# Opening products spread over eight places of the array, two fillers instead of 43, and a new step order in a delta-rule attention and expert-attention kernel

## The chip, the cores and the metric

The kernel runs on one core of a Trainium2 chip. The metric is device time in microseconds (us) of one execution. Three executions of the kernel before took 444.64, 447.53 and 451.43 us; the median is 447.53 us. Engines are named as the profile names them: PE (matrix products; PEld is its weight loads), DVE (vector), ACT (scalar), POOL (GpSimd) and SP (which issues the DMA transfers).

## The reference

The first half is a delta-rule recurrence over 768 tokens, for 4 batches and 8 heads of width 48. The second half takes its output as `x` and runs four experts of causal attention, with the two best gates of each token kept.

```python
k_n = k / (norm(k) + 1e-6)
for t in range(768):
    y[t]  = q[t] @ state
    state = state + beta[t] * outer(k_n[t], v[t] - k_n[t] @ state)
x = y, heads side by side: (4, 768, 384)
w = softmax over the two best of x @ w_gate
for e in range(4):
    q, k, v = x @ wq[e], x @ wk[e], x @ wv[e]        # width 64
    a = softmax(0.125 * q @ k.T, causal)
    out += gate[e] * (a @ v @ wo[e])
```

## The kernel before, in words

The recurrence is done in blocks. The work is cut into six units `n` (two pairs of batches by three stretches of 256 tokens), and each unit into four chunks `c` of 64 tokens. For one chunk, `gram` forms the products of the keys with themselves, and the triangular system that they make is solved for 64 tokens at a time. Unit 0 is solved in pieces of 16 rows on DVE and put together by products on PE (`gram_up`, `diag`, `expand`); the other units are solved in pieces of 32 rows on POOL and put together by `merge1` and `merge2`. Then the chain `ks, u, q, s, y` carries the state through the four chunks, and projections, scores, maxima, values and the output product of the experts follow (`pj, pv, mx, mp, mr, sc, av, nm, ft, fo`).

No scheduler orders the instructions. Every piece of work is a named step (`gr0.2` is `gram(0, 2)`, `sv0.9` is step 9 of the solve of unit 0), and the string `ORDER` lists them; the loop at L744 issues them in that order on all engines, and each engine runs its own instructions in the order in which they were issued. `+9` stands for nine fillers: products of a zero tile, 128 rows by 256 columns in bfloat16, that nobody reads.

The steps that the prediction follows are these. `load_k`, `load_q` and `load_chain` (`lg`, `lq`, `lc`) start transfers on SP. `gr0.c` is 32 float32 products on PE (L242) and two DVE operations that carry them out (L248). `si` (L273) transposes on DVE; `pre` (L289 to L310) prepares the solve; `sv0` (L335, L336) runs on DVE, `sv1` to `sv5` (L332, L333) on POOL after the product of L306. `so` (L353) and `sn` (L350) transpose the solved blocks back. `dg` (L360 to L363) places them with ACT and POOL, `ex` (L373) multiplies them on PE, `gq` (L267, L269) is the product of keys and queries, and `gu` (L256, L259) the part of the Gram product above the 16-row pieces, carried out by ACT. `gr1.c` is carried out by ACT (L246). All products share four PSUM banks in turn, the tiles `pm__66` to `pm__69`.

Before `ORDER` begins, PE runs one filler and `MINI` = 40 small float32 products, 48 rows by 32 columns with 4 columns moving, all into one place (L129). One float32 product is issued as two weight loads and two products, so four instructions; a filler is two.

Of the kernel before, what the change touches and what calls it, by code (L numbers as in the profile page):

```python
# [38 lines left out]
sv0.4 sv0.5 sv0.6 gu2 sv0.7 sv0.8 ks0.0 gu3 sv0.9 +4 gu0 sv0.10 sv0.11 sv0.12 sv0.13 +17 gr1.1 sv0.14 +2 gu1 sv0.16
vt0.1 so0 lq1.1 sn0 gr1.2 +5 gr1.0 si1 pre1.0 dg1 gq1.0 dg0 pre1.1 pre1.2 pre1.3 dg2 +62 ex1.0 +2 gq0.1 ex0.0 +9 ex2.0  # L40
ex1.1 ex0.1 pre1.4 gq0.0 dg3 sv1.1 sv1.2 sv1.3 +1 ex0.2 gq0.2 sv1.4 +2 ex0.3 kc3 cb sv1.5 sv1.6 ex1.2 u0.0 sv1.7 sv1.8
ex3.0 s0.0 sv1.9 ex1.3 ks0.1 w0 w4 y0.0 vs0 sv1.10 lc0.2 sv1.11 sv1.12 vt0.2 sv1.13 sv1.14 lq1.2 ex2.1 +9 q0.1 kc0
u0.1 ex2.2 s0.1 gq0.3 w1 w3 sv1.15 sv1.16 ks0.2 kc2 lc0.3 sv1.17 vt0.3 ex2.3 sv1.18 y0.1 lq1.3 ex3.1 sv1.19 sv1.20 w2
sv1.21 w6 hx0.1.0 sv1.22 +1 q0.2 lg2.1 u0.2 lq2.0 lg2.2 ex3.2 +1 s0.2 +7 ks0.3 lg2.3 y0.2 ex3.3 pv0.0.1 sv1.23 gq1.2
q0.3 lc1.0 sv1.24 sv1.25 lg2.0 sv1.26 u0.3 gr2.1 y0.3 hx0.3.0 sv1.27 gr2.2 gr2.3 sv1.28 sv1.29 sv1.30 +1 gr2.0 sv1.31
s0.3 si2 pj0.0.0 sv1.32 vt1.0 lc1.1 vt1.1 pj0.0.2 so1 mv1.1 sn1 pv0.1.0 q1.0 lq2.2 ks1.0 pre2.0 pre2.1 mv1.0 vs1 vs2
pj0.1.0 kc1 +5 m11.0 mv1.2 pre2.2 pre2.3 m11.1 mv1.3 cl1 pj0.1.2 pre2.4 sv2.1 sv2.2 sv2.3 m21.3 lg3.0 m21.0 w5 pv0.0.0
gq1.1 u1.0 m21.2 lq2.1 sv2.4 s1.0 sv2.5 mx0.1.1.1 m21.1 ks1.1 mx0.1.0.0 y1.0 mx0.0.1.1 gr3.0 sv2.6 sv2.7 sv2.8 mp0.1
sv2.9 u1.1 lc1.2 q1.1 lq2.3 vt1.2 +2 s1.1 sv2.10 mx0.0.0.0 mp0.0 gq2.0 lg3.1 mr0.1 ks1.2 mr0.0 y1.1 sv2.11 sv2.12
pv0.1.1 lc1.3 u1.2 sv2.13 hx1.1.0 sv2.14 sv2.15 sv2.16 q1.2 gq1.3 gr3.1 s1.2 gt0 vt1.3 sv2.17 sv2.18 sc0.0.0.0 sv2.19  # L50
sc0.0.1.0 lg3.2 lc2.0 ks1.3 sv2.20 sv2.21 lq3.0 y1.2 lg3.3 pj1.0.0 q1.3 u1.3 gq2.1 gq2.3 y1.3 sc0.1.0.0 gr3.3 +3 gq3.0
gr3.2 av0.0.0 si3 av0.0.1 av0.1.1 av0.0.3 pj1.0.2 hx1.3.0 +1 pj1.1.0 pv1.0.1 sv2.22 s1.3 av0.1.0 sv2.23 sv2.24 sv2.25
pre3.0 av0.0.2 sv2.26 sv2.27 pre3.1 mx1.0.0.0 pre3.2 sv2.28 sv2.29 sv2.30 sv2.31 pre3.3 pj1.1.2 sv2.32 so2 vt2.0
pv1.0.0 sn2 pre3.4 q2.0 ks2.0 sc0.1.1.0 mv2.0 lg4.0 sv3.1 pv1.1.1 sv3.2 m12.0 m12.1 cl2 sv3.3 nm0.0 mx1.0.0.1 mv2.1
pv1.1.0 m22.0 mx1.1.1.2 mv2.2 av0.1.3 sv3.4 u2.0 mx1.1.1.3 lc2.1 mv2.3 av0.1.2 s2.0 m22.2 lc2.2 vt2.1 sv3.5 nm0.1
m22.1 lq3.2 m22.3 sv3.6 sv3.7 sv3.8 mx1.0.1.2 vt2.2 ks2.1 sv3.9 sv3.10 sv3.11 ft0.0 mx1.0.1.3 sv3.12 sv3.13 y2.0 u2.1
lq3.1 mx1.1.0.1 mp1.0 fo0.0.0 q2.1 lq3.3 s2.1 mr1.0 fo0.0.1 sv3.14 sv3.15 sv3.16 gq2.2 gq3.1 ks2.2 lg4.2 y2.1 sv3.17
gr4.0 lc2.3 u2.2 vt2.3 lq4.2 sv3.18 mx1.1.0.0 sc1.0.0.1 hx2.1.0 ft0.1 q2.2 sv3.19 mp1.1 sv3.20 s2.2 sc1.0.0.0 sv3.21
sv3.22 sc1.0.1.0 gt1 sv3.23 ks2.3 y2.2 gr4.2 pv2.0.0 lg4.3 sv3.24 sv3.25 mr1.1 lg4.1 pj2.0.0 sv3.26 lc3.0 sv3.27 q2.3
u2.3 gr4.3 gq3.2 y2.3 hx2.3.0 fo0.1.1 gq3.3 gr4.1 av1.0.0 av1.0.1 sc1.0.1.1 si4 lq4.0 sv3.28 sv3.29 sv3.30 pj2.0.2  # L60
pj2.1.0 sv3.31 sv3.32 fo0.1.0 vt3.0 mx2.0.1.4 so3 av1.0.3 sn3 av1.0.2 lq4.1 sc1.1.0.0 mv3.2 sc1.1.0.1 pv2.0.1 mv3.1
m13.0 mx2.0.0.0 lc3.1 mv3.0 av1.1.0 m23.0 m23.1 pre4.0 pre4.1 m13.1 ks3.0 nm1.0 pre4.2 pre4.3 cl3 pre4.4 sc1.1.1.1
vt3.1 ft1.0 pj2.1.2 sv4.1 mv3.3 sv4.2 sv4.3 lg5.0 sv4.4 u3.0 gr5.0 s3.0 mx2.0.1.5 mx2.0.0.1 ks3.1 y3.0 m23.2 pv2.1.0
sv4.5 u3.1 mx2.1.1.5 sv4.6 sv4.7 mx2.0.0.2 mx2.0.0.3 q3.1 s3.1 lc3.2 sc1.1.1.0 mx2.1.1.4 vt3.2 ks3.2 sv4.8 sv4.9
sv4.10 lg5.1 y3.1 sv4.11 sv4.12 sv4.13 lg5.2 mx2.0.1.6 lc3.3 vt3.3 sv4.14 mx2.0.1.7 sv4.15 hx3.1.0 pv2.1.1 u3.2 gr5.1
sv4.16 q3.2 s3.2 lc4.0 mp2.0 sv4.17 sv4.18 mx2.1.1.6 av1.1.1 av1.1.2 av1.1.3 mr2.0 fo1.0.1 sc2.0.0.2 m23.3 ks3.3 lg5.3
gq4.1 y3.2 sc2.0.0.0 sc2.0.0.1 q3.3 u3.3 sv4.19 nm1.1 mx2.1.0.0 mx2.1.0.1 sv4.20 sv4.21 sv4.22 +1 y3.3 av2.0.1 av2.0.0
mx2.1.0.2 mx2.1.0.3 lq5.1 sc2.0.1.1 gr5.3 sv4.23 vt4.0 s3.3 gr5.2 gq5.1 ks4.0 mx2.1.1.7 mp2.1 sv4.24 sv4.25 sv4.26 si5
pre5.0 pre5.1 sc2.0.1.2 sc2.0.1.0 sv4.27 mr2.1 fo1.0.0 av2.0.2 sv4.28 sv4.29 sv4.30 sv4.31 pre5.2 av2.0.3 sc2.1.0.1
sv4.32 sc2.1.0.2 pre5.3 pre5.4 sv5.1 so4 pv3.0.0 pj3.0.0 hx3.3.0 mv4.0 ft1.1 mv4.1 sv5.2 sv5.3 lq5.0 sv5.4 pj3.1.0  # L70
sc2.1.0.0 lc4.1 mv4.2 sv5.5 sv5.6 sv5.7 sn4 m14.0 av2.1.0 sv5.8 sv5.9 sv5.10 av2.1.1 gt2 lq4.3 nm2.0 sc2.1.1.1
sc2.1.1.2 m24.0 m24.1 m14.1 cl4 sv5.11 sv5.12 sv5.13 sc2.1.1.0 pj3.0.2 sv5.14 pj3.1.2 vt4.1 u4.0 sv5.15 sv5.16 sv5.17
sv5.18 sv5.19 gq4.0 q4.0 s4.0 av2.1.2 av2.1.3 mx3.0.0.0 mx3.0.1.1 fo1.1.1 mp3.0 pv3.0.1 lc4.2 ks4.1 y4.0 gq4.2 u4.1
gq4.3 vt4.2 lq5.2 q4.1 mv4.3 sv5.20 sv5.21 s4.1 mr3.0 sv5.22 pv3.1.1 sv5.23 sv5.24 sv5.25 lq5.3 nm2.1 mx3.1.1.1
fo1.1.0 ks4.2 y4.1 m24.3 sv5.26 lc4.3 vt4.3 m24.2 ft2.0 pv3.1.0 sv5.27 sv5.28 sv5.29 sv5.30 hx4.1.0 u4.2 gq5.0 sv5.31
sv5.32 q4.2 s4.2 sc3.0.0.0 lc5.0 mx3.1.0.0 mp3.1 vt5.0 ks4.3 y4.2 pv4.0.1 fo2.0.0 fo2.0.1 ft2.1 pj4.0.2 gq5.2 so5 sn5
mv5.2 q4.3 mv5.0 u4.3 mr3.1 fo2.1.0 mv5.3 y4.3 hx4.3.0 s4.3 sc3.0.1.0 mv5.1 m15.1 m15.0 pj4.0.0 ks5.0 m25.0 m25.1
m25.3 gt3 pv4.0.0 pj4.1.0 pj4.1.2 q5.0 cl5 u5.0 mx4.0.1.3 lc5.1 vt5.1 sc3.1.0.0 m25.2 s5.0 mx4.0.0.1 av3.0.0 ks5.1
mx4.1.1.3 mx4.1.0.1 y5.0 u5.1 av3.1.0 sc3.1.1.0 mx4.0.0.0 lc5.2 q5.1 s5.1 av3.0.2 vt5.2 av3.0.3 lc5.3 av3.0.1 av3.1.2
vt5.3 nm3.0 av3.1.1 mx4.0.1.2 mp4.0 gq5.3 ks5.2 y5.1 hx5.1.0 pv4.1.0 fo2.1.1 mr4.0 pv4.1.1 u5.2 mx4.1.1.2 sc4.0.0.1  # L80
q5.2 s5.2 sc4.0.0.0 sc4.0.1.1 gt4 ks5.3 y5.2 ft3.0 pj5.0.0 q5.3 u5.3 mx4.1.0.0 mx5.0.0.0 y5.3 av4.0.0 mp4.1 hx5.3.0
av3.1.3 mx5.1.0.0 sc4.0.1.0 pj5.0.2 nm3.1 fo3.0.0 mr4.1 fo3.0.1 mx5.0.0.1 pj5.1.2 ft3.1 pj5.1.0 av4.0.1 mx5.0.1.6
sc4.1.0.1 av4.0.2 mx5.0.1.5 av4.0.3 mx5.0.0.2 sc4.1.0.0 sc4.1.1.0 mx5.0.0.3 av4.1.0 av4.1.1 mx5.0.1.4 sc4.1.1.1
mx5.0.1.7 mp5.0 nm4.0 pv5.0.0 fo3.1.1 mr5.0 fo3.1.0 ft4.0 pv5.1.0 mx5.1.0.1 av4.1.2 mx5.1.1.6 sc5.0.0.2 fo4.0.0
mx5.1.1.5 av4.1.3 sc5.0.0.1 sc5.0.0.0 fo4.0.1 nm4.1 mx5.1.1.4 mx5.1.1.7 av5.0.0 mx5.1.0.2 sc5.0.1.2 av5.0.1 mx5.1.0.3
mp5.1 sc5.0.1.0 sc5.0.1.1 ft4.1 pv5.1.1 mr5.1 pv5.0.1 gt5 av5.0.2 sc5.1.0.2 av5.0.3 sc5.1.0.0 sc5.1.0.1 fo4.1.0 nm5.0
av5.1.0 sc5.1.1.0 av5.1.1 sc5.1.1.1 sc5.1.1.2 fo4.1.1 ft5.0 av5.1.2 av5.1.3 fo5.0.1 fo5.0.0 nm5.1 ft5.1 +12 fo5.1.0
# [4 lines left out]
def tile_kernel(ctx, tc, kq, kv, beta, wqk, wvg, wo, consts, out):
# [24 lines left out]
    def mm(o, a, b, start, stop=True):  # L117
        T.matmul(o, lhsT=a, rhs=b, start=start, stop=stop, skip_group_check=True)  # L118
# [696 lines left out]
```

## Time and profile before

The profiled execution took 448.62 us; its span, from the first to the last instruction, is 446.9 us.

| | us | share of the span |
|---|---|---|
| median of three executions | 447.53 | |
| profiled execution | 448.62 | |
| its span | 446.9 | |
| PE busy | 423.3 | 95% |
| DVE busy | 277.2 | 62% |
| POOL busy | 256.8 | 57% |
| ACT busy | 203.5 | 46% |

PE is busy nearly everywhere, but a filler counts as busy too, and the ends of products are modelled. POOL works from 46 us to about 345 us, on the solves of units 1 to 5. The first 50 us hold the solve of unit 0, which only DVE runs, and little of what PE does there is on the path. A bracket at the end of a timeline row gives the idle time before it and what ended that; "issue" means that nothing that the profile shows was being waited for.

### The profile page before, as it was taken

What the parts mean: (1) busy time and instruction counts of PE and PEld (TensorE: products, weight loads), DVE (VectorE), ACT (ScalarE), POOL (GpSimd) and SP (SyncE); (2) the same over time, 40 slices, a digit from 0 to 9 for tenths busy, and PEclk for the clock granted to TensorE, in tenths of its full rate; (3) what the DMA queues carried; (4) which work ended last, traced back from release to release, by engine and by line L of the source; (5) the groups of instructions that cost most, each with busy time, mean ns of one, the idle gap of its engine ahead of it and who ended that gap; (6) DMA issues with size and microseconds to landing.
All of it is one profiled execution on the core that took longest, in us unless ns stands there. A gap on an engine that the chain in (4) does not pass through costs nothing.

```text
span 446.9 us, 24375 instructions
## 1 busy us (share of the span) xinstructions
PE 423.3 (95%) x10935; PEld 381.7 (85%) x10935; DVE 277.2 (62%) x615; ACT 203.5 (46%) x555; POOL 256.8 (57%) x477
## 2 busy tenths in 40 slices
...
PEclk9869998799999966999999999999999999999999
...
GB/s 273 209 4 4 5 155 130 106 103 76 87 127 23 60 3 86 158 90 75 91 62 116 70 27 96 4 32 132 88 37 49 68 38 33 24 38 38 1 29 81
...
## 3 DMA queue, kind: packets, MB, share of 16 engines
q1 hardware_dynamic: 18864, 31.18, 22.2%
q8 instruction: 86, 1.41, 1.3%
...
## 4 chain that ended last, share of the span: by engine, by line
PE 79%; DVE 14%; issue 4%; ACT 1%; POOL 1%; DVEq 0%; ACTq 0%; POOLq 0%
PE pm__66 L118 16%; PE pm__67 L118 15%; PE pm__68 L118 14%; PE pm__69 L118 13%; PE py L118 12%; PE xu L118 8%; DVE tt L353 1%; DVE B L273 1%; DVE B L276 1%; DVE tn L350 1%; DVE B L336 1%; DVE tm L335 1%; DVE rr L295 1%; PE pm__69 L672 1%; DVE g L290 1%
## 5 line engine op out<-in xcount | busy, mean ns | idle before, releaser
L333 POOL TENSOR_TENSOR B<-B,tm 128x30 f32<-128x30 f32 (+9 forms) x150 | 79.4, 529 | 11.8
L332 POOL TENSOR_TENSOR tm<-B 128x30 f32<-128x30 f32 (+9 forms) x150 | 74.4, 496 | 10.2
L640 POOL TENSOR_SCALAR_AFFINE_SELECT at<-at 128x256 f32<-128x256 f32 x48 | 19.4, 417 | 85.5 <-ACT at L638 74.8
L154 POOL TENSOR_TENSOR kv<-kv,nt 128x384 f32<-128x384 f32 x24 | 20.3, 849 | 33.5 <-DVE nt L301 18.3
L118 PE MATMUL py<-zb 128*128 128x256 bf16 (+1 forms) x279 | 34.4, 270 | 3.1 <-DVE h L481 1.5
L118 PEld LDWEIGHTS <-zb 128*128 128x128 bf16 x199 | 20.0, 107 | 8.6 <-issue 2.6
L118 PE MATMUL py<-qf,sb 48*48 48x64 f32 x704 | 25.1, 222 | 1.8 <-DVE h L481 0.9
L118 PEld LDWEIGHTS py<-qf,sb 48*48 48x48 f32 x704 | 21.9, 123 | 4.1 <-DVE h L481 1.3
L478 ACT ACTIVATE xh<-py 112x384 fp32r<-112x384 f32 x24 | 11.8, 491 | 21.4 <-PE py L118 21.1
L447 ACT ACTIVATE ub<-xu 128x384 f32<-128x384 f32 x24 | 11.8, 492 | 20.3 <-PE xu L118 17.2
L395 POOL COPY tt<-tt 32x256 f32<-32x256 f32 x40 | 15.7, 392 | 8.9 <-DVE tt L353 7.5
L585 DVE TENSOR_REDUCE mx<-pm__67 128x1 f32<-128x512 f32 (+3 forms) x26 | 16.2, 623 | 7.3 <-PE pm__68 L118 6.4
L585 DVE TENSOR_REDUCE mx<-pm__69 128x1 f32<-128x512 f32 (+3 forms) x22 | 13.5, 614 | 9.6 <-PE pm__66 L118 8.7
L480 DVE TENSOR_TENSOR xh<-py,xh 112x384 fp32r<-112x384 f32 x24 | 13.2, 552 | 9.9 <-ACT h L479 9.2
L459 DVE TENSOR_TENSOR sb<-sb,xu 112x384 f32<-112x384 f32 x20 | 11.0, 551 | 12.8 <-PE xu L118 12.4
L585 DVE TENSOR_REDUCE mx<-pm__68 128x1 f32<-128x512 f32 (+3 forms) x25 | 15.8, 630 | 4.9 <-PE pm__69 L118 4.9
L118 PE MATMUL xu<-xs,tt 64*64 64x48 f32 x768 | 17.8, 228 | 0.7 <-POOL tt L410 0.7
L118 PE MATMUL py<-pm,ub 64*48 64x64 f32 x768 | 17.0, 222 | 1.1 <-issue 0.9
L118 PE MATMUL pm__68<-QHI,KHI 64*128 64x256 f32 (+1 forms) x54 | 16.5, 306 | 0.6 <-DVE lg L530 0.6
L306 POOL TENSOR_TENSOR B<-B,nn 128x1024 f32<-128x1024 f32 x5 | 11.9, 2384 | 8.6 <-DVE nn L303 7.6
L118 PEld LDWEIGHTS xu<-xs,tt 64*64 64x64 f32 x768 | 15.0, 142 | 2.1 <-POOL tt L410 1.0
L276 DVE STREAM_TRANSPOSE B<-tt 32x1024 f32<-32x1024 f32 x8 | 16.4, 2045 | 0.2
...
## 6 DMA issues: line engine op xcount, KB each, us to landing
...
```

The source lines that it names most:

```text
L118: T.matmul(o, lhsT=a, rhs=b, start=start, stop=stop, skip_group_check=True)
L154: G.tensor_tensor(vt, vt, PR[n]["nt"][:, c * NP:c * NP + NP, None].to_broadcast([128, NP, HD]), op=OP.mult)
L276: V.transpose(B[r:r + 32], gf[r:r + 32, :, 0:32].rearrange("p t j -> p j t"))
L306: G.tensor_tensor(pr["B"], pr["B"], nn[:, None, :].to_broadcast([128, 32, 32]), op=OP.mult)
L332: e.tensor_tensor(tv, bc(Z[:, i:i + 1, i + 1:]), bc(Z[:, 0:i, i:i + 1]), op=OP.mult)
L333: e.tensor_tensor(Z[:, 0:i, i + 1:], Z[:, 0:i, i + 1:], tv, op=OP.add)
L395: G.tensor_copy(o[r:r + 32, :, 0:32], o[r:r + 32, :, 32:64])
L447: S.activation(eight(UB), PX, AF.Copy)
L478: S.activation(hi, Y[:, :, 0:3], AF.Copy)
L480: V.tensor_tensor(lo, Y[:, :, 0:3], hi, op=OP.subtract)
L585: V.tensor_reduce(dst.rearrange("p (y x) -> p x y", x=2)[:, x, y:y + per], P[x], axis=AX.X, op=OP.max)
L640: G.affine_select(d, d, pattern=[[0, 2], [1, 128]], compare_op=OP.is_ge, fill=0.0, base=0, channel_multiplier=-1)
```

## The change

The 40 opening products are the same in number and size. Each now starts its own sum, and they go in turn over two halves of the rows and four groups of 32 columns of the array, so eight places, into two banks. The order string is replaced as a whole; its first lines of before and after stand here.

```diff
-+43 gr0.0 +4 gr0.1 +4 gr0.3 gr0.2 si0 pre0.0 pre0.1 pre0.2 pre0.3 pre0.4 vt0.0 lc0.1 sv0.1 lq1.0 sv0.2 sv0.3 gr1.3
++2 gr0.0 +4 gr0.2 gr0.3 gr0.1 si0 pre0.0 lq1.0 pre0.1 pre0.2 kc1 pre0.3 pre0.4 sv0.1 +4 gr1.3 cb sv0.2 sv0.3 gu3 kc3
...
     zf = ZB.bitcast(F32)
-    for _ in range(MINI):
-        mm(PY0[0:32, 0, 256:260], zf[0:HD, 0:32], zf[0:HD, 0:4], False)
+    for k in range(MINI):
+        r, c = k % 2, 32 * (k // 2 % 4)
+        mm(PY0[c:c + 32, r, 256:260], zf[64 * r:64 * r + HD, 0:32], zf[64 * r:64 * r + HD, 0:4], True)
```

The string holds 198 fillers before and 175 after. Lines of the changed file are two higher than those of before from L130 on.

On PE, at the first Gram product: before, the end of the 43 fillers and the first rows of `gr0.0` (its keys are the tile kf_114).

```order
L118 MATMUL py<-zb 128x256
L118 LDWEIGHTS zb
L118 MATMUL py<-zb 128x256
L118 LDWEIGHTS zb
L118 MATMUL py<-zb 128x256
L118 MATMUL pm__67<-kf_114 32x32 x4
L118 MATMUL pm__68<-kf_114 32x32 x4
```

After, the opening products, the two fillers and `gr0.0`.

```order
L118 MATMUL py<-zb 32x4 x40
L118 LDWEIGHTS zb
L118 MATMUL py<-zb 128x256
L118 LDWEIGHTS zb
L118 MATMUL py<-zb 128x256
L118 MATMUL pm__67<-kf_114 32x32 x4
L118 MATMUL pm__68<-kf_114 32x32 x4
```

Of the 43 pairs ahead of the Gram product two are left, so 82 instructions fewer stand there.

On PE, behind the Gram products of unit 0 (kf_115 to kf_117 are chunks 1 to 3 of unit 0, kf_121 is chunk 3 of unit 1): before, the end of `gr0.3`, `gr0.2`, then `gr1.3`.

```order
L118 MATMUL pm__68<-kf_117 32x32 x4
L118 MATMUL pm__69<-kf_116 32x32 x4
L118 MATMUL pm__66<-kf_116 32x32 x4
L118 MATMUL pm__69<-kf_116 32x32 x4
L118 MATMUL pm__66<-kf_116 32x32 x4
L118 MATMUL pm__69<-kf_116 32x32 x4
L118 MATMUL pm__66<-kf_116 32x32 x4
L118 MATMUL pm__69<-kf_116 32x32 x4
L118 MATMUL pm__66<-kf_116 32x32 x4
L118 MATMUL pm__67<-kf_121 32x64 x4
```

After, the end of `gr0.1`, four fillers, then `gr1.3`.

```order
L118 MATMUL pm__69<-kf_115 32x32 x4
L118 MATMUL pm__66<-kf_115 32x32 x4
L118 LDWEIGHTS zb
L118 MATMUL py<-zb 128x256
L118 LDWEIGHTS zb
L118 MATMUL py<-zb 128x256
L118 LDWEIGHTS zb
L118 MATMUL py<-zb 128x256
L118 LDWEIGHTS zb
L118 MATMUL py<-zb 128x256
L118 MATMUL pm__67<-kf_121 32x64 x4
```

The chunk that comes last of unit 0 is now chunk 1, and no filler stands between the last three.

On DVE, in the middle of the solve of unit 0 (`tm` and `B_181` are its two operations of a step): before, steps 8 to 10.

```order
L335 TENSOR_TENSOR tm<-B_181 128x112
L336 TENSOR_TENSOR B_181<-B_181,tm 128x2x8x7
L335 TENSOR_TENSOR tm<-B_181 128x108
L336 TENSOR_TENSOR B_181<-B_181,tm 128x2x9x6
L335 TENSOR_TENSOR tm<-B_181 128x100
L336 TENSOR_TENSOR B_181<-B_181,tm 128x2x10x5
```

After, the same steps, with the product of keys and queries of chunk 1 between (`gq0.1`, tile `pm`).

```order
L337 TENSOR_TENSOR tm<-B_181 128x112
L338 TENSOR_TENSOR B_181<-B_181,tm 128x2x8x7
L337 TENSOR_TENSOR tm<-B_181 128x108
L338 TENSOR_TENSOR B_181<-B_181,tm 128x2x9x6
L271 TENSOR_TENSOR pm<-pm__67,cst 128x256
L271 TENSOR_TENSOR pm<-pm__68,cst 128x256
L337 TENSOR_TENSOR tm<-B_181 128x100
L338 TENSOR_TENSOR B_181<-B_181,tm 128x2x10x5
```

Two DVE operations that stood behind the solve of unit 0 now stand inside it.

More of the change, by code (lines that the diff above doesn't have):

```diff
@@ L37 @@
 ORDER = """
-+43 gr0.0 +4 gr0.1 +4 gr0.3 gr0.2 si0 pre0.0 pre0.1 pre0.2 pre0.3 pre0.4 vt0.0 lc0.1 sv0.1 lq1.0 sv0.2 sv0.3 gr1.3
[L39 to L87, printed above, removed]
@@ L88 @@
-fo5.1.1
++2 gr0.0 +4 gr0.2 gr0.3 gr0.1 si0 pre0.0 lq1.0 pre0.1 pre0.2 kc1 pre0.3 pre0.4 sv0.1 +4 gr1.3 cb sv0.2 sv0.3 gu3 kc3
+sv0.4 sv0.5 sv0.6 sv0.7 sv0.8 gu1 lc0.1 vt0.1 +16 gu0 sv0.9 vt0.0 ks0.0 +6 gq0.1 +3 gu2 +21 gr1.0 gr1.1 +1 gr1.2
+sv0.10 sv0.11 sv0.12 sv0.13 sv0.14 sv0.16 so0 sn0 dg1 si1 pre1.0 gq0.0 lq1.2 dg0 pre1.1 pre1.2 pre1.3 lq1.1 dg2 pre1.4
+sv1.1 +47 ex1.0 +2 gq1.0 ex0.0 kc2 sv1.2 +9 ex1.1 ex0.1 sv1.3 sv1.4 sv1.5 sv1.6 w1 ex2.0 sv1.7 sv1.8 ex1.2 dg3 ex0.2
++7 ex0.3 ex2.1 w3 ex1.3 u0.0 +5 s0.0 gq1.2 w2 sv1.9 sv1.10 ks0.1 y0.0 +1 u0.1 sv1.11 sv1.12 gq0.2 +2 q0.1 s0.1 lc0.2
@@ new lines @@
+vt0.2 sv1.13 sv1.14 sv1.15 sv1.16 sv1.17 w0 ex2.2 lc0.3 ex3.0 vt0.3 +6 ex2.3 ks0.2 y0.1 ex3.1 w4 q0.2 sv1.18 u0.2
+lq1.3 sv1.19 sv1.20 sv1.21 ex3.2 s0.2 gq0.3 lg2.1 hx0.1.0 ks0.3 sv1.22 sv1.23 sv1.24 lg2.2 sv1.25 lg2.0 y0.2 ex3.3
+pv0.0.0 vs1 w5 sv1.26 q0.3 u0.3 lc1.0 gr2.1 gr2.2 y0.3 lg2.3 gr2.3 sv1.27 sv1.28 sv1.29 lq2.1 gr2.0 sv1.30 si2 pj0.0.2
+s0.3 hx0.3.0 pj0.0.0 pre2.0 lc1.1 pv0.0.1 pj0.1.0 q1.0 sv1.31 sv1.32 so1 sn1 vt1.0 ks1.0 lg3.0 vt1.1 mv1.3 mv1.0
+pj0.1.2 pre2.1 mv1.2 lq2.2 pre2.2 pre2.3 m11.1 m11.0 pv0.1.1 m21.2 +1 m21.0 mv1.1 m21.1 cl1 pre2.4 sv2.1 sv2.2 sv2.3
```

41 lines of the change are left out of this document (added).

## The prediction

> **What bounds the kernel now.** First the page's busy shares and its clock row, then windows over the stages.
>
> ```profile
> PE 423.3 (95%) x10935; PEld 381.7 (85%) x10935; DVE 277.2 (62%) x615; ACT 203.5 (46%) x555; POOL 256.8 (57%) x477
> PEclk9869998799999966999999999999999999999999
> 45.00:85.00 40.00, 34.17 (x1218) 31.47 (x1220) 22.65 (x46) 14.28 (x36) 34.68 (x62) 0.95 0.34 107
> 85.00:345.00 260.00, 251.82 (x6865) 229.03 (x6857) 180.21 (x372) 124.40 (x335) 201.18 (x366) 0.96 0.24 73
> ```
>
> From 85 us on PE is busy for 97% (251.82 of 260), so whatever brings that stage forward brings the end forward. From 45 to 85 us POOL is busy 34.68 of 40 us with the solve of unit 1, and PE is idle for 5.8. Ahead of that stands the solve of unit 0. I read it in the timelines of PE, DVE and POOL (start, duration, engine, and in brackets the idle time before).
>
> ```profile
> 1.46 4.34 PEld L118 LDWEIGHTS py<-zb 48*32 48x32 f32 x80 [0.22 <-issue]
> 5.81 6.23 PEld L118 LDWEIGHTS <-zb 128*128 128x128 bf16 x43
> 12.25 0.12 PEld L118 LDWEIGHTS pm__67<-kf 48*32 48x32 f32 x4 [0.21 <-issue]
> 12.94 0.61 PE L118 MATMUL py<-zb 128*128 128x256 bf16 x4
> 13.48 0.12 PEld L118 LDWEIGHTS pm__69<-kf 48*32 48x32 f32 x4 [0.21 <-issue]
> 19.06 0.23 PE L118 MATMUL pm__66<-kf 48*32 48x32 f32 x3 [3.35 <-issue]
> 19.44 0.33 PE L118 MATMUL pm__67<-kf 48*32 48x64 f32 x4
> 20.54 0.37 PE L118 MATMUL pm__69<-kf 48*64 48x64 f32 x2
> 20.09 1.94 DVE L273 STREAM_TRANSPOSE B<-tt 128x1024 f32<-128x1024 f32 x1
> 35.93 1.97 DVE L353 STREAM_TRANSPOSE tt<-B 128x1024 f32<-128x1024 f32 x1
> 39.56 1.88 DVE L273 STREAM_TRANSPOSE B<-tt 128x1024 f32<-128x1024 f32 x1
> 46.17 2.36 POOL L306 TENSOR_TENSOR B<-B,nn 128x1024 f32<-128x1024 f32 x1 [1.25 <-DVE nn L303]
> ...
> 22.30:33.50 11.20, 10.25 (x258) 7.34 (x258) 10.07 (x38) 6.87 (x29) 1.61 (x2) 0.67 0.01 4
> ```
>
> PE spends 4.34 us on the opening products and 6.23 on 43 fillers; the first Gram product starts at 12.25. In the middle of the fourth, PE stands still for 3.35 us and waits for nothing that the profile shows. Then DVE runs `si0` at 20.09, the solve, `so0` at 35.93 and `si1` at 39.56, busy for 10.07 of the 11.2 us of the last row, a window within it, and POOL can begin unit 1 at 46.17. So the start of `si0` sets the first 46 us.
>
> What was the standstill? The instruction transfers and the counts say it.
>
> ```profile
> q8 instruction: 86, 1.41, 1.3%
> 0.00:18.00 18.00, 14.58 (x350) 12.20 (x351) 1.63 (x7) 1.49 (x2) 6.01 (x16) 1.00 0.86 298
> 18.00:22.00 4.00, 2.59 (x128) 2.23 (x127) 2.40 (x3) 0.66 (x2) 0.00 (x0) 0.68 0.03 8
> 22.73 0.37 PE L118 MATMUL pm__69<-kf 48*64 48x64 f32 x1 [1.07 <-issue]
> q8 instruction: 1, 0.02, 4.9%
> q8 instruction: 1, 0.02, 5.2%
> ```
>
> PE's 21,870 instructions over 86 packets are 254 each. PE stopped after 350 + 351 = 701 of them, and again after 128 + 127 = 255 more. The last two rows are from the windows 16.6 to 17.8 and 20.3 to 21.4: one packet each, followed by PE's restart at 19.06 and 22.73. So I take it that instructions come in blocks of 256 whose edges lie at 189, 445, 701 and so on, and that passing an edge asks for the block after the next one. From 19.06 to 22.73 that took 3.7 us. Edge 445 lies 61 of 128 instructions into the second Gram product, which starts at 13.48, so at about 13.8; its block let PE go on at 19.06, which is 5.3 us, while the data transfers kept the queues full (0.86).
>
> **The opening products and the fillers.** Forty products on one place take 4.34 us, 108 ns each. The 32 Gram products from 12.25 to 12.94, which already alternate over eight places, take 0.69 us, 22 ns each. Forty at that price are 0.9 us, and with one place as the other bound 4.34; I take 1.2, for PE is slow at its start (the windows from 5.80 and 9.20, below). The 41 fillers take 6.23 × 41/43 = 5.9 us away. What is late next is the keys.
>
> ```profile
> 0.82 0.39 SPq L141 DMA_DIRECT2D kf<-in_kq_dram  x1
> 1.72 1.38 SPq L141 DMA_DIRECT2D kf<-in_kq_dram  x3
> DMA to landing us min/median/max: 2.8/3.6/4.4
> ```
>
> These four issues and their landings, 2.8 to 4.4 us behind them (a window around them alone), put chunk 0 at 3.6 us and the last of unit 0 at 7.1 (2.7 + 4.4). Their place in SP's queue doesn't change.
>
> **When `si0` starts.** Ahead of `gr0.0` stand 2 + 160 + 4 = 166 instructions, so edge 189 falls just inside it, at 3.8 us. The block from 445 arrives 3.7 to 5.3 us later, at 7.5 to 9.1. Edge 445 falls 15 instructions into the third Gram product (166 + 128 + 8 + 128 = 430), and the fourth ends at 686, ahead of edge 701. So the Gram products of unit 0 no longer meet the edge on which PE stood for 3.35 us. The 241 instructions left cost 0.69 us for 128 (12.25 to 12.94) or 1.1 cold (19.44 to 20.54), so 1.3 to 2.1 us; the eviction and the step to `si0` cost 0.65 (19.44 to 20.09). `si0` starts at 9.4 to 11.8; I take 10.6, the middle, since cold products and a full queue both are likely. The gain is 8.3 to 10.7, say 9.5.
>
> [...]
>
> **What the new order adds to this path.** `gq0.1` now stands inside the solve.
>
> ```profile
> 42.41 0.42 DVE L269 TENSOR_TENSOR pm<-pm__67,cst 128x256 f32<-128x256 f32 x1
> 42.74 0.41 DVE L269 TENSOR_TENSOR pm<-pm__68,cst 128x256 f32<-128x256 f32 x1
> 38.41 0.30 POOL L361 MEMSET tt<- 32x256 f32 x1 [11.78 <-ACT tt L360]
> 48.71 0.39 POOL L362 COPY VS<-tn 32x256 f32<-32x256 f32 x1
> ```
>
> Its two operations start 0.33 us apart: 0.7 us on DVE ahead of `so0`. Gain of `si1` and of POOL's L306: 9.5 − 0.7 = 8.8. Their PE products must come in time: block 957 arrives at 7.5 to 9.1 plus two cycles, 15 to 20 us, and DVE gets there at about 22; if that cover goes, all of DVE's chain slips with it. `dg3` (48.46 to 49.9) moves on POOL from ahead of `sv1.1` to behind `sv1.8`: 1.5 us sooner for the one, given back later, so nothing. `vt0.1` is multiplied before `vt0.0`: POOL is idle for 11.78 us there, nothing. On SP, `lq1.2` waits for `gq0.0`, and the weight loads `w1`, `w3`, `w2` queue behind it, at about 28 us; before, two of them went out at 14. ACT asks for them only among the `ex` steps; were it sooner, ACT would wait some 5 us.
>
> **PE up to `ex`.**
>
> ```profile
> 26.03 3.80 PE L118 MATMUL py<-zb 128*128 128x256 bf16 x17
> 35.05 6.94 PE L118 MATMUL py<-zb 128*128 128x256 bf16 x62
> 41.92 1.15 PE L118 MATMUL pm__69<-VS 64*64 64x64 f32 x32
> 26.00:28.00 2.00, 2.00 (x14) 1.42 (x11) 1.90 (x6) 2.00 (x10) 0.62 (x1) 0.50 0.00 0
> 5.80:9.20 3.40, 3.40 (x18) 2.41 (x17) 0.00 (x0) 0.00 (x0) 0.96 (x2) 1.00 1.00 342
> 9.20:12.05 2.85, 2.85 (x28) 2.56 (x26) 0.00 (x0) 0.00 (x0) 0.00 (x0) 1.00 1.04 391
> ```
>
> A filler takes 0.22 us at clock 0.50 (17 in 3.80) and 0.11 at 1.00 (62 in 6.94). `gr1.2` ends at instruction 1620, in the block from 1469, which arrives at 22 to 27 us by the cycle above; with `gq0.0` the 47 fillers start at about 28. At half of each price they take 7.8 us (bounds 5.3 and 10.5): `ex1.0` starts at 35.8 (33.1, where `sn0` frees its input, to 38.5) against 41.92, a gain of 6.1 (3.4 to 8.8).
>
> **The sum.** POOL's path gains 8.8, PE's 6.1. From 45 us on POOL is the busier, so I stay near its value: 8.0. The profiled execution goes from 448.6 to 440.6; it lay 1.1 above the median, so the median goes from 447.5 to 439.5. Later steps are in another order but the same work, and 198 − 175 = 23 fillers fewer are, beside the first 41, 18 more elsewhere (2 us), where I let them hide PE's waits.
>
> **Rivals.** (a) *More:* `si0` at the early end (10.7) and the idle 5.8 us of 45 to 85 half filled: 447.5 − 10.7 − 2.9 = 434. The kernel before loses that time in waits that another order may cover; nothing shows that it does. (b) *The order gives it back:* the waits move. One such:
>
> ```profile
> 67.14 2.28 issue
> 70.00:75.00 5.00, 5.00 (x126) 4.62 (x125) 2.92 (x4) 1.43 (x3) 4.68 (x7) 0.66 0.20 41
> ```
>
> It is followed by a clock of 0.66 over 5 us, so costs 2.3 + 0.34 × 5 = 4.0 us. One or two more of them and it is 443.5 to 447.5. (c) *Slower, by the clock:* the rows 5.80 and 9.20 show 18 fillers in 3.40 us and then 28 in 2.85: the array was slow until about 9 us, whatever the clock column says there, and became fast under the fillers. Without them it is still slow when the blocks of unit 0 are put together. At 1.1/0.69 = 1.6 times the time for a product, the 34.17 busy us of 45 to 85 would cost 20 more: 459.5. From 13 us of busy PE at half clock (8.0/0.6) it is slower than before, from 28 (17/0.6) by over 2%. Against it: 47 fillers in a row stand ahead of `ex1.0`.
>
> [...]
>
> (d) *The places don't help:* the 40 products still take 4.34 us. Then the first Gram product starts at 6.2 (1.46 + 4.34 and two fillers), the block from 445 comes at 10 to 11.6, `si0` starts at 12.0 to 14.3, and 2.6 us of gain are gone: 442.
>
> **Numbers.** The forecast has 0.50, its own range 435 to 444; (a) 0.20, (b) 0.14, (c) 0.10, (d) 0.06. A measurement here tells about 2% from no change, so faster is below 438.6: (a) and a little under half of the forecast, 0.43. Slower, above 456.5: most of (c) and a tail of (b), 0.09. The rest is 0.48. The range leaves out the lower half of (a) and (c): 433 to 448.
>
> **What would show it.** `si0` at 9.4 to 11.8 and `so0` at about 27; no standstill of PE within the Gram products of unit 0, but one behind them near instruction 701; L306 on POOL near 37 and `ex1.0` near 36. If those hold and the end doesn't move, (b) is right, and new idle rows on PE behind 45 us show it; a PEclk row of 5s behind 36 us shows (c). `gr0.0` later than 5 us shows (d). If `si0` starts near 10 and the standstill is gone altogether, my blocks are wrong.

## The result, and the profile after

The changed kernel takes 433.04 us (median of six executions, 431.29 to 438.03) against 446.68 us before (six, 444.64 to 451.43). The ratio is 0.969, with a 95% interval of 0.963 to 0.975: faster by 3.1%. Times here are medians of all executions, ratios compare undisturbed executions only, and the kernel before is taken anew on each chip. The forecast was 439.5 us, so a gain of 8.0; it came out at 13.6, at the lower end of the range that was given (433 to 448). The profiled execution took 431.71 us with a span of 430.0.

The page of the changed kernel, busy shares and clock:

```profile
PE 406.0 (94%) x10912; PEld 365.6 (85%) x10912; DVE 275.9 (64%) x615; ACT 202.8 (47%) x555; POOL 257.2 (60%) x477
PEclk9999999899999999999999999999999999999999
```

Its timelines at the places that the prediction spoke of (lines are two higher than before), from queries by engine and put in order of time:

```profile
1.46 0.86 PEld L118 LDWEIGHTS py<-zb 48*32 48x32 f32 x80 [0.22 <-issue]
3.76 0.28 PE L118 MATMUL pm__67<-kf 48*32 48x32 f32 x4 [0.81 <-DMA kf<-in_kq_dram]
8.95 0.28 PE L118 MATMUL pm__68<-kf 48*32 48x32 f32 x4 [1.00 <-DVE tt L250]
10.94 1.90 DVE L275 STREAM_TRANSPOSE B<-tt 128x1024 f32<-128x1024 f32 x1
14.65 0.32 PE L118 MATMUL pm__67<-kf 48*32 48x64 f32 x3 [2.77 <-issue]
27.42 2.04 DVE L355 STREAM_TRANSPOSE tt<-B 128x1024 f32<-128x1024 f32 x1
31.13 1.88 DVE L275 STREAM_TRANSPOSE B<-tt 128x1024 f32<-128x1024 f32 x1
34.72 1.15 PE L118 MATMUL pm__67<-VS 64*64 64x64 f32 x32
37.74 2.35 POOL L308 TENSOR_TENSOR B<-B,nn 128x1024 f32<-128x1024 f32 x1 [1.25 <-DVE aa L312]
```

The opening products take 0.86 us, not 4.34. The first Gram product starts at 3.76 and waits for its keys. In the third, PE stands for 1.00 us until 8.95, after 223 + 223 = 446 instructions, so at edge 445. The row puts this wait down to DVE, but DVE's operations on these two tiles had ended at 5.1; by the prediction the block from 445 arrives at 7.5 to 9.1. The instruction queue moved one packet between 6.6 and 6.8 us, some 2.2 us ahead of that restart, and the next between 12.0 and 12.3, ahead of the restart at 14.65. `si0` starts at 10.94, and PE's standstill of 2.77 us now lies behind the Gram products of unit 0, in `gr1.3`. `so0`, `si1`, `ex1.0` and POOL's first product of unit 1 start at 27.42, 31.13, 34.72 and 37.74, where the prediction had 27, 31, 35.8 and 37.4. Against before they are 8.5, 8.4, 7.2 and 8.4 us sooner. Up to here it holds.

But the gap doesn't stay at 8.4. The starts of `si` (L273 before, L275 after), unit by unit, in the two profiled executions:

| unit | 0 | 1 | 2 | 3 | 4 | 5 | end of span |
|---|---|---|---|---|---|---|---|
| before | 20.1 | 39.6 | 89.4 | 139.1 | 202.7 | 261.8 | 446.9 |
| after | 10.9 | 31.1 | 78.1 | 125.4 | 183.8 | 240.1 | 430.0 |
| sooner by | 9.2 | 8.4 | 11.3 | 13.7 | 18.9 | 21.7 | 16.9 |

(Some 3 us of the last column are the profiled executions' own distance from their medians, 448.62 against 446.68 and 431.71 against 433.04.) The later stages gained too, and that is what the prediction had put at nothing. It wasn't the idle time of 45 to 85 us either, on which rival (a) rested: in the changed kernel PE is idle there for 5.8 us again.

```profile
45.00:85.00 40.00, 34.20 (x1153) 31.66 (x1149) 22.87 (x38) 12.23 (x30) 34.92 (x61) 0.96 0.34 108
```

### The profile page after: what moved, and what is told of

Read it like the earlier page. It is cut to its first block, busy times and chain, and to the rows that moved or that the text cites. A ratio compares the mean times of both kernels' runs of the same rounds, so it can differ in the third digit from the quotient of the medians.

```text
span 430.0 us, 24315 instructions
## 1 busy us (share of the span) xinstructions
PE 406.0 (94%) x10912; PEld 365.6 (85%) x10912; DVE 275.9 (64%) x615; ACT 202.8 (47%) x555; POOL 257.2 (60%) x477
## 4 chain that ended last, share of the span: by engine, by line
PE 73%; DVE 13%; POOL 4%; issue 4%; DMA 2%; ACT 1%; SPq 1%; DVEq 0%; ACTq 0%
PE pm__69 L118 15%; PE pm__67 L118 15%; PE pm__68 L118 12%; PE py L118 12%; PE pm__66 L118 11%; PE xu L118 7%; DVE B L278 3%; POOL B L335 2%; POOL tm L334 2%; DVE B L275 1%; DMA kf<-in_kq_dram 1%; DVE tt L355 1%; DVE tn L352 1%; DMA xh<-h 1%; SPq L489 1%
## 5 line engine op out<-in xcount | busy, mean ns | idle before, releaser
L335 POOL TENSOR_TENSOR B<-B,tm 128x30 f32<-128x30 f32 (+9 forms) x150 | 80.7, 538 | 11.8
L118 PE MATMUL py<-zb 128*128 128x256 bf16 (+1 forms) x256 | 27.1, 264 | 2.7 <-DVE h L483 1.6
L480 ACT ACTIVATE xh<-py 112x384 fp32r<-112x384 f32 x24 | 11.8, 492 | 19.7 <-PE py L118 19.6
L118 PEld LDWEIGHTS <-zb 128*128 128x128 bf16 x176 | 16.5, 103 | 5.2 <-DVE zb L123 1.1
L587 DVE TENSOR_REDUCE mx<-pm__66 128x1 f32<-128x512 f32 (+3 forms) x28 | 17.3, 617 | 4.7 <-PE pm__67 L118 3.2
L118 PE MATMUL pm__67<-xh,wqkh 128*128 128x256 f32 x108 | 19.9, 284 | 0.0
L587 DVE TENSOR_REDUCE mx<-pm__67 128x1 f32<-128x512 f32 (+3 forms) x25 | 16.0, 640 | 5.8 <-PE pm__68 L118 5.8
L461 DVE TENSOR_TENSOR sb<-sb,xu 112x384 f32<-112x384 f32 x20 | 11.0, 550 | 10.4 <-PE xu L118 10.3
L118 PE MATMUL pm__67<-kf 48*64 48x64 f32 (+2 forms) x304 | 12.0, 245 | 5.7 <-issue 4.9
L118 PE MATMUL xu<-xs,tt 64*64 64x48 f32 x768 | 16.7, 221 | 0.5 <-DVE xs L443 0.5
L118 PEld LDWEIGHTS xu<-xs,tt 64*64 64x64 f32 x768 | 14.0, 134 | 3.5 <-issue 1.7
L118 PEld LDWEIGHTS pm__67<-xh,wqkh 128*128 128x128 f32 x108 | 16.5, 188 | 0.3 <-DVE QLO L515 0.2
L118 PEld LDWEIGHTS pm__67<-kf 48*32 48x32 f32 (+1 forms) x304 | 9.6, 140 | 7.7 <-issue 5.5
```

Of the source, the lines that this page charges most:

```text
L335: e.tensor_tensor(Z[:, 0:i, i + 1:], Z[:, 0:i, i + 1:], tv, op=OP.add)
L461: V.tensor_tensor(eight(new), eight(state(n, c)), SP, op=OP.add)
L480: S.activation(hi, Y[:, :, 0:3], AF.Copy)
L587: V.tensor_reduce(dst.rearrange("p (y x) -> p x y", x=2)[:, x, y:y + per], P[x], axis=AX.X, op=OP.max)
```

## The experiments

**The two halves of the change.** `start_only` is the kernel before with the new opening alone.

```diff
-    for _ in range(MINI):
-        mm(PY0[0:32, 0, 256:260], zf[0:HD, 0:32], zf[0:HD, 0:4], False)
+    for k in range(MINI):
+        r, c = k % 2, 32 * (k // 2 % 4)
+        mm(PY0[c:c + 32, r, 256:260], zf[64 * r:64 * r + HD, 0:32], zf[64 * r:64 * r + HD, 0:4], True)
-+43 gr0.0 +4 gr0.1
++2 gr0.0 +4 gr0.1
```

> The kernel before with the new opening alone: the 40 products over eight places and 2 fillers ahead of the first Gram product, the rest of the order as it was. Theory 1 (the opening is worth its 8.5 us, and the other 5 us of the measured gain come from elsewhere in the order): si0 at 10 to 12 us, ratio to before 0.981 (438 us). Rival (the gain is the order's): 0.99 or more. Rival (the opening does it all): 0.969.

It took 455.2 us, ratio 1.017 (0.998 to 1.036), although `si0` started at 11.6 and POOL's L306 at 37.7, as in the changed kernel. `order_only` is the other half: the changed kernel with the old opening lines and `+43`.

> The changed kernel with the old opening: 40 products on one place and 43 fillers ahead of the first Gram product. Theory 1: si0 near 20 us as in the kernel before, since the last Gram product crosses the edge at instruction 701 again, and the ratio to before is 0.987 (441.5 us), the order's own 5 us. Rival (the opening does it all): 1.00.

447.9 us, ratio 1.001 (0.996 to 1.006). All three theories fell: one half gains nothing and by its median costs, the other does nothing, and together they gain 3%. So the two are not terms of a sum. The waits of PE in the two kernels show what `start_only` lost. First before, then `start_only` (columns: us in total, times, longest).

```profile
PE pm__66 L118 <- issue: 5.6, 2, 3.3
PE pm__69 L118 <- issue: 3.7, 4, 1.7
...
PE py L118 <- issue: 2.2, 3, 0.9
```

```profile
PE xu L118 <- issue: 5.4, 7, 1.1
PE py L118 <- issue: 4.7, 5, 2.2
PE pm__67 L118 <- issue: 4.2, 2, 3.1
PE pm__69 L118 <- issue: 3.8, 5, 2.2
```

With the smaller rows, such waits come to 12.1 us before and to 20.2 in `start_only`, and they changed their place. Before, they lie mostly at the tiles `pm__66` and `pm__69`, and only 2.2 us at `py`; in `start_only` 10.1 us lie at `xu` and `py`. But for 1.0 us at a filler (0.5 before), that is the state chain (`ks`, `u`, `q`, `s`, `y`), whose every product waits for the one before. PE's timelines show single ones, before first:

```profile
69.42 0.80 PE L118 MATMUL pm__66<-tt,up 64*64 64x64 f32 x20 [2.28 <-issue]
...
83.56 0.27 PE L118 MATMUL pm__69<-kf 48*64 48x64 f32 x1 [1.74 <-issue]
```

```profile
62.94 0.49 PE L118 MATMUL xu<-sb,kf 48*64 48x48 f32 x18 [0.63 <-issue]
...
67.76 0.76 PE L118 MATMUL py<-qf,sb 48*48 48x64 f32 x20 [0.67 <-issue]
80.25 0.33 PE L118 MATMUL py<-pm,ub 64*48 64x64 f32 x8 [2.19 <-issue]
```

That gave theory E: 82 instructions fewer at the start move every later edge of the 256-instruction blocks by 82 instructions, here into the chain.

**The edges by themselves.** Four kernels tell E from theory O (the old order was fitted to the old times). A helper issues small products like the opening ones, four instructions each, and `~n` in the order string calls it.

```diff
+    def tiny(n):
+        for k in range(n):
+            r, c = k % 2, 32 * (k // 2 % 4)
+            mm(PY0[c:c + 32, r, 256:260], zf[64 * r:64 * r + HD, 0:32], zf[64 * r:64 * r + HD, 0:4], True)
```

`start_aligned`: the 82 instructions are put back into `start_only`, ahead of `ex1.0`.

```diff
-dg2 +62 ex1.0
+dg2 ~20 +63 ex1.0
```

> The kernel before with the new opening, as start_only, and 82 instructions put back ahead of the 62 fillers (20 of the small products over eight places and one filler), so that all later instructions stand at the same places against the edges of the 256-instruction blocks as in the kernel before. Theory E (start_only lost its 8.5 us because the later edges moved by 82 instructions into dense stretches): PE's idle time put down to issue falls from 20 us to near the 12 us of before, and the ratio to before is 0.98 to 0.99. Theory O (the old order was fitted to the old times of its waits): stays at 1.01 to 1.02.

438.9 us, ratio 0.986 (0.981 to 0.991): 82 instructions more, and 16 us less than `start_only` (14 by the ratios). They take nothing away on the spot: `ex1.0` starts at 37.73 us, in `start_only` at 37.62. The waits are near those of before in size, 12.6 us, and only 3.6 of them lie at `py` and `xu`:

```profile
PE pm__67 L118 <- issue: 5.0, 2, 3.1
PE py L118 <- issue: 3.4, 4, 1.2
...
PE pm__69 L118 <- issue: 2.5, 3, 1.8
```

Against before, `start_aligned` starts its six `si` 8.2, 8.2, 6.9, 7.7, 11.6 and 9.7 us sooner and ends 9.3 us sooner. So the opening's lead is carried to the end. What the changed kernel has beyond that begins between `si1` and `si2`: 0.3 us at `si1`, 4.4 at `si2`, 6.0 at `si3`, 7.6 at the end. (These are single executions; `after_again`, the changed kernel profiled once more, lies up to 3.2 us behind its first profile.)

`before_shift` and `after_shift` do the reverse to the kernel before and to the changed one.

```diff
-dg2 +62 ex1.0          (before)
+dg2 ~32 +56 ex1.0
-sv1.1 +47 ex1.0        (changed)
+sv1.1 ~32 +41 ex1.0
```

> The kernel before with the same 116 instructions more ahead of ex1.0 (32 small products in the place of 6 of the 62 fillers). Theory E, where the old order was fitted to its edges: 4 to 10 us slower, ratio 1.01 to 1.022. Theory O, or edges without weight: 1.00.

455.1 us, ratio 1.019 (1.010 to 1.028).

> The changed kernel with 116 instructions more ahead of ex1.0 at the same time (32 small products over eight places in the place of 6 of the 47 fillers), which moves every later edge by nearly half a block. Theory E: 4 to 10 us slower than the changed kernel, ratio to before 0.977 to 0.99. Theory O: as the changed kernel, 0.966 to 0.97.

442.6 us, ratio 0.994 (0.991 to 0.998), where the changed kernel has 0.969. So each kernel loses some 9.5 us. But a good part of it is lost on the spot, and not at the later edges. In `after_shift`:

```profile
31.03 8.01 PE L118 MATMUL py<-zb 48*32 48x4 f32 x87 [1.55 <-issue]
32.00:34.00 2.00, 2.00 (x12) 1.43 (x10) 1.90 (x5) 1.90 (x5) 1.60 (x5) 0.50 0.81 278
38.98 1.15 PE L118 MATMUL pm__67<-VS 64*64 64x64 f32 x32
```

PE stands among the small products, after 860 + 860 = 1,720 instructions, and behind that the granted clock is 0.50 (third column from the right), at which a filler takes about twice its time (in the kernel before, 17 took 3.80 us at 0.50, and 62 took 6.94 at 1.00). `ex1.0` starts at 38.98, 4.3 us later than in the changed kernel. In `before_shift` PE stands after the same 1,720 instructions, for 1.76 us, and `ex1.0` starts 4.8 us later than before. That leaves some 5 us of each loss to what comes later. The waits of the changed kernel, and then of `after_shift`:

```profile
PE pm__67 L118 <- issue: 4.9, 2, 2.8
...
PE py L118 <- issue: 2.0, 4, 0.6
...
PE pm__66 L118 <- issue: 1.3, 2, 0.8
```

```profile
PE py L118 <- issue: 4.8, 5, 1.5
PE pm__67 L118 <- issue: 3.3, 2, 2.7
PE xu L118 <- issue: 2.4, 3, 1.2
PE pm__68 L118 <- issue: 2.3, 2, 1.4
```

With the smaller rows they grow from 8.7 to 14.7 us. The 1.55 us on the spot are among the 4.8 at `py`; the other 4.4 us of growth come later, much of it again at `py` and `xu`, and are near the 5 us that are left. So these two runs are weaker evidence for later edges than `start_only` against `start_aligned`, where nothing is lost on the spot.

`order_aligned` is `order_only` with 41 fillers fewer in the stretch where DVE solves unit 0.

```diff
-gu1 lc0.1 vt0.1 +16 gu0 sv0.9 vt0.0 ks0.0 +6 gq0.1 +3 gu2 +21 gr1.0
+gu1 lc0.1 vt0.1 gu0 sv0.9 vt0.0 ks0.0 gq0.1 +3 gu2 +2 gr1.0
```

> The changed kernel with the old opening (one place, 43 fillers), as order_only, but with 41 fillers fewer ahead of gr1.0, where DVE is still solving, so that all later edges lie as in the changed kernel. Theory E: the order then keeps its own gain, ratio 0.98 to 0.99 (the changed kernel and 8.5 us). Theory O: as order_only, 1.00.

443.1 us, ratio 0.993 (0.989 to 0.997). The direction is E's, but the size is half: its `si0` starts at 18.7, and the new order brings 2.5 us there, not 5. It is no clean test, either: without the 41 fillers the granted clock is 0.50 from 22 to 38 us, and `ex1.0` starts at 43.1, later than before (41.9).

**Small shifts.** `after_p32` has 32 instructions more, `after_m32` 16 fillers fewer.

```diff
-sv1.1 +47 ex1.0
+sv1.1 ~8 +47 ex1.0     (after_p32)
+sv1.1 +31 ex1.0        (after_m32)
```

> The changed kernel with 32 instructions more ahead of ex1.0 (8 small products, 0.2 us). If the changed order is fitted closely to its edges: 3 us or more slower than the changed kernel, ratio to before 0.975 or more. If only large shifts matter: 0.966 to 0.972.

444.0 us, ratio 0.995 (0.988 to 1.002). Here `ex1.0` starts at 36.30, as in `after_again` (36.18), so the loss lies behind it: the waits come to 13.8 us, one of them 2.3 us at `xu`.

> The changed kernel with 16 fillers of the 47 ahead of ex1.0 left out, so 32 instructions fewer, and PE reaches ex1.0 up to 1.8 us sooner. If the order is fitted closely to its edges: slower in spite of the earlier ex1.0, 0.975 or more. If the 47 fillers hold PE back, as the sum of the prediction has it: 1 to 2 us faster, 0.962 to 0.968.

434.3 us, ratio 0.980 (0.973 to 0.986), 1 us from the changed kernel. Thirty-two instructions one way cost most of the gain, 32 the other way next to nothing. The ratio of `after_m32` would fit its first expectation (0.975 or more), but the changed kernel itself had 0.984 in another set (`after_again`, below), so here the times decide: neither expectation came true. PE reached `ex1.0` no sooner in a way that counted (34.5 us, where the changed kernel has 34.7; L308 at 39.3, as in `after_again`, 39.2). The new order fits its edges, but not on a knife's edge on both sides.

**The edge inside the Gram products.** `mini44` and `mini0` change the number of opening products in the changed kernel, with one execution each.

```diff
-MINI = 40
+MINI = 44              (mini44)
+MINI = 0               (mini0)
```

> The changed kernel with 44 opening products in the place of 40, so 16 instructions and about 0.1 us more. The last Gram product of unit 0 then ends at instruction 702, one past the edge. Theory E: si0 waits for the block from 701, which lands at 14.4 us in the changed kernel, and starts at about 15 us in the place of 10.9. Rival (no edges): 11.0.

PE and DVE in `mini44`:

```profile
10.26 0.31 PE L118 MATMUL pm__66<-kf 48*32 48x32 f32 x5
13.97 0.21 PE L118 MATMUL pm__66<-kf 48*32 48x32 f32 x1 [3.40 <-issue]
...
14.54 1.96 DVE L275 STREAM_TRANSPOSE B<-tt 128x1024 f32<-128x1024 f32 x1
```

One single instruction of the fourth Gram product stands behind the edge, after 350 + 351 = 701 others. It alone is held for 3.40 us, and `si0` starts at 14.54, 3.6 us late, for four products that take 0.09 us.

> The changed kernel without the opening products, so 160 instructions and about 1 us less work. Theory E: the first edge is passed 47 instructions into the second Gram product, about 6.7 us, in the place of 3.8; the block from 445 comes at 10.4 to 12, and si0 starts at 12.2 to 14.5, later than with the products. Rival (the products only cost time): 10.9 or sooner.

```profile
12.59 0.21 PE L118 MATMUL pm__69<-kf 48*32 48x32 f32 x1 [3.15 <-issue]
0.00:12.50 12.50, 4.57 (x222) 3.25 (x223) 1.63 (x7) 1.49 (x2) 6.01 (x16) 1.00 0.82 272
...
13.71 1.98 DVE L275 STREAM_TRANSPOSE B<-tt 128x1024 f32<-128x1024 f32 x1
```

Here PE stands after 222 + 223 = 445 instructions, at the edge before. Without the products `si0` starts at 13.71, 2.8 us later than with them; in the other profiles that keep the changed kernel's opening and Gram products it starts at 10.4 to 11.5. So what the products do here is not work but count: with these 160 cheap instructions, 0.86 us in all, PE goes on behind edge 445 at 8.95 us, and without them at 12.59. That passing the first edge early asks for the next block early is the prediction's reading, which fits both times; the rows of `mini0` don't show the transfer itself. The executions took 437.55 and 440.9 us.

**The two parts of the opening, with edges kept.** `old_mini` puts the 40 products of the changed kernel back on one place (the two old lines), with no instruction more or fewer.

> The changed kernel with the 40 opening products on one place again, as before; no instruction more or fewer, so all edges lie as in the changed kernel. By the prediction's rival (d): the first Gram product at 6.2 us, si0 at 12.0 to 14.3 in the place of 10.9, and 1 to 3 us slower than the changed kernel, ratio 0.972 to 0.977. If the places don't matter: 0.969.

`si0` starts at 13.2, and it takes 435.2 us, ratio 0.984 (0.974 to 0.994): 2.2 us above the changed kernel's 433.04. The four executions, 433.7 to 438.7, overlap with the changed kernel's, so the start is clear and the price is not. `fill43_aligned` has 43 fillers again, and the same 41 fewer behind the Gram products as `order_aligned`.

> The changed kernel with 43 fillers in the place of 2 ahead of the first Gram product, and 41 fillers fewer behind the Gram products of unit 0, so that the edges behind gr1.0 lie as in the changed kernel. The last Gram product then ends at instruction 768, behind the edge at 701. Theory E: first Gram product at 9, si0 at 15 to 17 us, 4 to 6 us slower than the changed kernel, ratio 0.978 to 0.983. If only the fillers' own time counted (first Gram product at 9, then 3 us to si0 at 12 to 13): 0.972.

`si0` at 17.8, later than expected, and 441.3 us, ratio 0.993 (0.988 to 0.998), so 8 us for a `si0` that is 6.8 us late. `ex1.0` and L308 are 6.6 us late as well. Here too the granted clock is 0.50 from 18 to 34 us.

**The fillers ahead of `m12` and `m22`.** The new order has two groups of 7 there, where the kernel before ran at a granted clock of 0.51 from 159 to 176 us. `after_no7` leaves them out; `before_7` gives them to the kernel before.

```diff
-+7 m12.0 m12.1 cl2 nm0.0 +7 m22.0      (changed)
+m12.0 m12.1 cl2 nm0.0 m22.0
-m12.0 m12.1 cl2 sv3.3 nm0.0 mx1.0.0.1 mv2.1 pv1.1.0 m22.0      (before)
++7 m12.0 m12.1 cl2 sv3.3 nm0.0 mx1.0.0.1 mv2.1 pv1.1.0 +7 m22.0
```

> The changed kernel without the two groups of 7 fillers ahead of the merge products of unit 2 (m12, m22). Theory (these fillers keep the array's clock up over the wait for so2, where the kernel before ran at 0.50 for 17 us): a granted clock of 0.50 from about 150 us for 7 to 17 us, and 3 to 6 us more than the changed kernel, ratio to before 0.976 to 0.983. Rival (the fillers do nothing): 14 fillers of 0.11 us fewer, 1.5 us faster or the same, 0.966 to 0.969.

> The kernel before with 7 fillers ahead of m12 and 7 ahead of m22, as the changed kernel has them. Theory (clock): no stretch at 0.50 from 159 to 176 us, 4 to 6 us less than before, ratio 0.987 to 0.991. Rival (they do nothing here): 1.00 to 1.004.

`after_no7` took 437.4 us, ratio 0.983 (0.978 to 0.989), and has the slow stretch again; `before_7` lost its stretch but took 444.6 us, ratio 0.999 (0.992 to 1.005). The windows of 155 to 160 us of `after_no7`, of the changed kernel and of `before_7`; the third column from the right is the granted clock:

```profile
155.00:160.00 5.00, 5.00 (x117) 4.01 (x116) 2.31 (x6) 0.77 (x2) 4.48 (x12) 0.50 0.36 110
```

```profile
155.00:160.00 5.00, 4.97 (x179) 4.04 (x178) 4.77 (x12) 2.43 (x6) 4.46 (x11) 1.00 0.76 227
```

```profile
155.00:160.00 5.00, 4.78 (x151) 4.24 (x150) 4.90 (x12) 2.68 (x5) 4.51 (x11) 1.00 0.03 8
```

Both kernels also move their later edges by 28 instructions, which by then was a cause of its own. `after_tiny7` takes the fillers' time and keeps the count; `after_again` is the changed kernel beside it.

```diff
-+7 m12.0 m12.1 cl2 nm0.0 +7 m22.0
+~3 m12.0 m12.1 cl2 nm0.0 ~4 m22.0
```

> The changed kernel with 3 and 4 small products in the place of the two groups of 7 fillers ahead of m12 and m22: the same 28 instructions, so all edges as in the changed kernel, but 0.15 us of work in the place of 1.9. If after_no7 lost its 4.4 us to the clock: a stretch at 0.50 from about 151 us again, and 3 to 5 us slower than the changed kernel of the same job. If it lost them because its edges moved by 28: no slower than the changed kernel.

> The changed kernel itself, beside after_tiny7 on the same chip: ratio to before 0.966 to 0.975.

435.0 us (ratio 0.986, 0.975 to 0.997) and 433.5 us (0.984, 0.975 to 0.993). The changed kernel repeats its time (433.0), but its ratio missed the 0.966 to 0.975 that was expected, because the kernel before doesn't repeat: its executions in this set go from 438.5 to 450.3 us. So a ratio can move by 1.5% from one set to the next for one and the same kernel, and the 3.1% of the change has that uncertainty as well. In `after_tiny7` the small products start sums of their own in the tile in which the chain's sums are kept, so its output is not the kernel's; the rest of the work is the same. Its clock falls to 0.61 and 0.71 in the windows where the changed kernel has 1.00:

```profile
150.00:155.00 5.00, 4.63 (x107) 3.42 (x108) 2.46 (x6) 2.70 (x6) 4.65 (x9) 0.61 0.01 3
155.00:160.00 5.00, 5.00 (x129) 3.81 (x127) 3.48 (x8) 1.37 (x3) 4.46 (x11) 0.71 0.52 157
```

So the clock stays up there with the fillers (1.00) and not without their time (0.61 and 0.71), but that is worth at most some 1.5 us here (435.0 against 433.5), and with four executions each, 432.8 to 435.2 against 431.6 to 434.9, this isn't told from nothing. The other 2.4 us of `after_no7` came with the 28 instructions or with its longer slow stretch, which is not separated. No long standstill of PE lies ahead of the drops in `after_no7` and `after_tiny7`: in the 5 us before them PE is shown idle for at most 0.65 us at a time, and in `after_tiny7` it is busy for 4.49 us from 145 to 150 us. What brings the clock down there is not shown.

`start_7a` and `start_7b` add the 14 fillers to `start_aligned`, with the edges 28 instructions off behind `m22` or ahead of `m12`.

```diff
-dg2 ~20 +63 ex1.0
+dg2 ~27 +49 ex1.0      (start_7a)
+dg2 ~20 +49 ex1.0      (start_7b)
-m12.0 m12.1 ... pv1.1.0 m22.0
++7 m12.0 m12.1 ... pv1.1.0 +7 m22.0
```

> start_aligned with the 14 fillers ahead of m12 and m22, and 14 fillers ahead of ex1.0 exchanged for 7 small products, so that the edges lie as before up to m12 and 28 instructions off behind m22. If opening, edges and clock add up: 6.7 and 4.5 us below before, ratio 0.975, all but 1 to 2 us of what the changed kernel gains, with the old order. If 28 instructions off already cost: 0.98 to 0.99.

> The same without the 7 small products: the edges lie 28 instructions off up to m12, and as before behind m22. If the three add up and the stretch behind m22 is where edges matter: 0.975. If the state chain of units 0 and 1 is hit by the shift: 0.98 to 0.99.

439.6 us (0.985, 0.976 to 0.995) and 438.6 us (0.982, 0.972 to 0.992): no faster than `start_aligned`, with wide intervals. Opening, edges and clock don't simply add, and no mixture of the old order with the new opening came near the changed kernel.

## Why the prediction was wrong, and where it was right

The step that failed is the last one of the sum, which put everything behind 45 us at nothing: the new order, and the edges that it moves. What came ahead of it held.

**Right: the path up to 45 us.** That `si0` sets the first 46 us; the edges at 445 and 701, 256 instructions apart (PE stood after 446 instructions in the changed kernel and after 445 in `mini0`, and after 701 before and in `mini44`; no row shows a standstill at 189); the price of the opening products (0.86 us, for an estimate of 0.9 to 1.2); PE going on behind edge 445 at 8.95, within the 7.5 to 9.1 of its block; `si0` at 10.94 within 9.4 to 11.8; and the long standstill moved behind the Gram products. Within them only the 1.00 us at edge 445 is left, which the working had in its block from 445 and its list of signs had not. `mini44` and `mini0` are the proof of the edges: 16 instructions more or 160 fewer delay `si0` by 3.6 and 2.8 us.

**Rival (d)** didn't come, since the places did help, but its working was right. With them undone in `old_mini`, PE goes on behind edge 445 at 11.23 (10 to 11.6 was given) and `si0` moves to 13.2 (12.0 to 14.3). The price, 2.2 us for 2.6, is not told from the spread.

**Right in direction: the opening's worth.** With the old order and the edges kept, it gains 6.7 us (445.58 to 438.91 in `start_aligned`) where the sum had 8.0; there 63 fillers hold `ex1.0`, not 47.

**Wrong: "Later steps are in another order but the same work".** This step put the new order behind 45 us at nothing. Of the 13.6 us measured the opening explains 6.7, which leaves about 7 to the order. That split depends on which half is put in first: with the old opening the order brought 2.5 us (`order_aligned`), which leaves some 10 to the opening, though with a slow clock in the way. Either way the order isn't nothing. Hardly any of it is a term that could have been added. One was in sight: the fillers ahead of `m12` and `m22` stood in the change, beside a slow clock row that stood in the page (the two sixes that hold 159 to 176 us); but they bring 1.5 us at most. I read the new fillers' number (198 and 175) and not their places.

**Wrong by what was left out: the edges behind unit 0.** I used the blocks for the four Gram products and then dropped them, though by the same count the change moves every later edge by 82 instructions and more. That has a price of its own: 14 to 16 us (`start_only` against `start_aligned`), some 11 us by the medians (`after_p32`), and about 5 us behind `ex1.0` in `before_shift` and `after_shift`. By the prediction's own working, `start_only` would have been 8 us faster than before; by its median it was 6.4 slower. That the sum came out with the right sign rests on the new order standing well against its new edges, which nothing in the prediction had looked at; so far it was luck.

**Rivals (a), (b) and (c).** The time is that of (a), 434, but not by its mechanism: `si0` was not at the early end, and the idle time of 45 to 85 us was not filled. (b), waits that move, is what happened in `start_only` and `after_p32`, by the edges; in `start_only` with the drop of the clock that (b) describes (0.62 and 0.70 from 80 to 90 us, behind the wait of 2.19 us), in `after_p32` without one behind its longest wait. (c) didn't come: the clock row of the changed kernel holds no stretch of 5s.

**Open.** How the 7 us of the order divide between fewer waits and better placed edges can't be told: with the edges moved by 32 instructions the way of `after_p32` most of the gain goes, and no run has the new order without edges. That the order has some worth beside its edges is likely, not shown: with the new opening and moved edges the new order had 0.994 and 0.995 (`after_shift`, `after_p32`), the old one 1.017 (`start_only`).
